# A fused attention, mixture and channel-mix kernel: the order of issue from a table in the source in place of the framework's scheduler

## The chip, the cores and the metric

The kernel runs on one core of a Trainium2 chip. The metric is the device time of one execution in microseconds (us), the median of several runs. Less is better.

## The reference

Three layers follow each other, with 4 batches, 544 rows per batch (32 "global" and 512 "local") and a model width of 512.

1. Attention with 8 heads of width 64. The 32 global queries see all 544 keys. A local query sees the 32 global keys and the local keys at most 32 places away.
2. A mixture of 4 experts, each a causal attention with its own `wq`, `wk`, `wv` of width 64 and an output weight `wo`. A gate picks the best two of four experts for each row and weighs them.
3. A channel mix: with `xk` and `xr` as blends of each row and the row before it, the result is `sigmoid(xr @ w_r) * (relu(xk @ w_k)**2 @ w_v)`, with a hidden width of 1024.

```
s = where(abs(i - j) <= 32, q_l @ k_l.T / 8, -1e9);  out_l = softmax([q_l @ k_g.T / 8, s]) @ [v_g, v_l]
x = concat([out_g, out_l]).transpose(0, 2, 1, 3).reshape(B, S, H * D)
ye = softmax(causal(scale * (x @ wq[e]) @ (x @ wk[e]).T)) @ (x @ wv[e]) @ wo[e]      # e = 0..3
x = sum over the two chosen experts of weight * ye
out = sigmoid(xr @ w_r) * (maximum(xk @ w_k, 0) ** 2 @ w_v)
```

All inputs and the output are float32.

## The kernel before, in words

The transposed activations `xT` of all four batches stay in SBUF. Precise products are made of three matmuls on a high and a low part (`mm3`, lines 112 to 114), plain float32 matmuls appear in the trace as two instructions each.

**Stage A** (lines 220 to 376) is the first attention. It goes over 32 half units `n`, a pair of heads and half of its queries each. `a_qk` makes scores S in eight matmuls on half of the array's rows each: head `h` = 0 uses rows 0 to 63, head 1 rows 64 to 127, and the program lists them in turns. VectorE (DVE) takes them out with a mask and a row minimum, ScalarE (ACT) makes the exponential, GpSimd (POOL) normalizes (`a_norm`), TensorE (PE) transposes (`a_tp`) and multiplies by the values (`a_pv`). For every fourth `n`, `g_qk` makes the scores of the global queries: for each pair and head a matmul of 512 columns into `Sga` and one of 32 columns into `Sgb`.

**Stage B/C** (from line 878, with `c_step`) is the mixture. `b_split` splits half a batch of `xT` into high and low parts in the one buffer `x`; `b_qk` and `b_v` make q, k and v of it. Then for each of 8 units per batch `c_qk` makes causal scores C of 128 to 512 columns (again in turns between the two row halves), DVE takes them out, ACT makes the exponential, POOL scales, PE transposes into `cT`, ACT and DVE copy that to `cpt`, and `c_pv` multiplies by the values into `y`. `e_wo` applies `wo` (tile `po`). Between these steps the 20 weight splits of the third layer (`load_wd`, `split_wd`) are placed, each with work on ACT, POOL and DVE.

**Stage D** is the channel mix over five blocks of tokens: `d_mix` makes blends on ACT, DVE and POOL; `d_k`, `d_v` and `d_r` are long runs of 128x512 matmuls; `d_out` multiplies and stores.

In the kernel before, the code only traces the operations. The framework's scheduler, with a model of time inside, then sets the order in which each engine issues them, and the allocator gives buffers in that order. At some places `tc.issue_after` ties an operation behind another one on its engine (`with after(last_act):` and the like). An engine issues its own instructions in order: one that waits for a semaphore holds up all behind it on that engine. The scores' and transposes' PSUM tiles share six buffers, `x` has one, most others two to four.

Of the kernel before, what the change touches and what calls it, by code (L numbers as in the profile page):

```python
# [23 lines left out]
W = 160  # L24
# [21 lines left out]
def v32(ap):  # L46
    return ap.bitcast(F32)


@with_exitstack  # L50
def chain_kernel(ctx: ExitStack, tc: tile.TileContext, kq, vw, vgd, wqkv, pack, wo, w_k, w_v, w_r, c_causal, out):
    nc = tc.nc

    const = ctx.enter_context(tc.tile_pool(name="const", bufs=1))
    sb = ctx.enter_context(tc.tile_pool(name="sb", bufs=1))
    xpool = ctx.enter_context(tc.tile_pool(name="xpool", bufs=1))
    tiny = ctx.enter_context(tc.tile_pool(name="tiny", bufs=1))
    ps = ctx.enter_context(tc.tile_pool(name="ps", bufs=1, space=PSUM))
    dr = ctx.enter_context(tc.tile_pool(name="dr", bufs=1, space=bass.MemoryType.DRAM))


# [93 lines left out]
    def split_wd(name, raw, c, k):  # L155
        lo, hi, hf = raw[:, :, 0], raw[:, :, 1], v32(raw)[:, :, 1]
        y = T("wy", [512], f"wy{name}{c}{k}", U32)
        g = T("wg", [512], f"wg{name}{c}{k}", U32)


        with after(last_act):
            nc.scalar.activation(v32(g), hf, AF.Sign, bias=tcol)
            nc.scalar.activation(v32(y), hf, AF.Abs)
        with after(last_pool):
            nc.gpsimd.tensor_scalar(v32(y), v32(y), TINY, None, op0=ALU.max)
        with after(last_dve):
            nc.vector.tensor_scalar(y, y, 3, 0x7fffffff, op0=ALU.logical_shift_left, op1=ALU.bitwise_and)
        nc.vector.scalar_tensor_tensor(g, lo, 29, g, op0=ALU.logical_shift_right, op1=ALU.bitwise_or)
        nc.vector.scalar_tensor_tensor(y, y, 0x7f800000, g, op0=ALU.bitwise_xor, op1=ALU.bitwise_xor)
        if name == "k":  # L170
            if (name, k) not in wd:
                for s in "HL":
                    place_wd(name, k, s)
            H_, L_ = [t[c % 4] for t in wd[name, k]]
        else:
            H_, L_ = g.bitcast(F32R), y.bitcast(F32R)
        nc.scalar.copy(H_, v32(y))
        nc.gpsimd.tensor_sub(L_, v32(y), v32(H_))
        if name != "k":
            for s, t in zip("HL", (H_, L_)):  # L180
                nc.sync.dma_start(wdr[name, k, s][:, c % 4], v32(t))
# [14 lines left out]
    def split_wb(step, c):  # L196
        kind = "qkv"[step]
        r = wraw[kind][:, c]
        H_, L_ = [t[:, c] for t in wqk[kind]]
        with after(last_act):  # L200
            nc.scalar.copy(H_, r)
        return lambda: nc.gpsimd.tensor_sub(L_, r, v32(H_))


# [27 lines left out]
        vws[P] = t  # L232

    def a_qk(n):
        nonlocal last_act, last_dve
# [12 lines left out]
        su = T("su", [4], f"su{n}", F32, 4)  # L248
        for i in range(2):
            k = 2 * j + i  # L250
            m = 0 if k == 0 else (2 if k == NB - 1 else 1)
            for h in range(2):
                c = 2 * h + i
                last_dve = nc.vector.tensor_tensor_reduce(out=ts[:, h, i], in0=st[h][:, i * W:(i + 1) * W],  # L254
                                                          in1=band[:, m], op0=ALU.add, op1=ALU.min, scale=-SCALE,
                                                          scalar=BIG, accum_out=mn[:, c:c + 1])
                last_act = nc.scalar.activation(ts[:, h, i], ts[:, h, i], AF.Exp, bias=mn[:, c:c + 1], scale=-1.0,  # L257
                                                accum_out=su[:, c:c + 1])
        sm[n] = ts
        rs[n] = su  # L260

    def a_norm(n):
        nonlocal last_pool
# [13 lines left out]
        g = glob[u][:, 2 * j:2 * j + 2, 2 * pp:2 * pp + 2, :].rearrange("p i h c -> p h i c")  # L277
        rb = rc.rearrange("p (h i) -> p h i", h=2)[:, :, :, None].to_broadcast([128, 2, 2, SG])
        last_pool = nc.gpsimd.tensor_tensor(g, t[:, :, 64:96].rearrange("p (h i) c -> p h i c", h=2), rb, op=ALU.mult)
        pn[n] = o  # L280

    def a_tp(n):
# [99 lines left out]
        return lambda: split_wo(raw)  # L382

    def split_wo(raw):
        with after(last_act):
            nc.scalar.copy(woS[0], raw)
        with after(last_pool):
            nc.gpsimd.tensor_sub(woS[1], raw, v32(woS[0]))
# [113 lines left out]
    csm, crs, cpt, ptl = {}, {}, {}, {}  # L502

    def c_qk(b, ep, i):
        nonlocal last_act
        w = 128 * (i + 1)
        q = qk[b, ep]
        rc = slice(i * 128, (i + 1) * 128)
# [16 lines left out]

    def c_norm(b, ep, i):
        w = 128 * (i + 1)
        nonlocal last_dve, last_pool
# [4 lines left out]
        last_dve = nc.vector.tensor_mul(rc, rc, gate[b][:, i, 2 * ep:2 * ep + 2])  # L533
        for e in range(2):
            t = csm[b, ep, i][e]
            last_pool = nc.gpsimd.tensor_tensor(t[:, :w], t[:, :w], rc[:, e:e + 1].to_broadcast([128, w]),  # L536
                                                op=ALU.mult)

    def c_tp(b, ep, i):
        nonlocal last_act, last_dve  # L540
        ts = csm.pop((b, ep, i))
        pt = T("cpt", [2, NB, 160], f"cpt{b}{ep}{i}")
        for e in range(2):
# [236 lines left out]
    def c_step(m):  # L780
# [27 lines left out]
        if m == MIX:  # L808
            d_begin()
        if MIX <= m < MIX + NC:  # L810
            with after(last_act), after(last_dve), after(last_pool):
                d_mix(0, 0, [m - MIX])
        if m >= K0 and m < K0 + FIRST:
            d_k(0, m - K0)
        if jobs and m >= J0 and (m - J0) % 4 < 3:
# [20 lines left out]
    for n in range(NU + 6):  # L836
        if n == 5:
            nc.sync.dma_start(small, pack)
        if n == 14:
            ql = T("ql", [2, 2, 128], "ql", F32R)  # L840
            qld = [[ql[:, p, s] for s in range(2)] for p in range(2)]
            with after(last_pool):
                nc.gpsimd.memset(v32(ql), 0.0)
            with after(last_dve):
                nc.vector.tensor_scalar(omu, mu, -1.0, 1.0, op0=ALU.mult, op1=ALU.add)
        u, r = divmod(n, 4)
        with after(last_pool):
            for g in low:
                g()
        low = []  # L850
        if n < NU:
            a_qk(n)
# [49 lines left out]
    for n, (g0, w) in enumerate(tokens):  # L902
# [24 lines left out]
        else:  # L927
# [78 lines left out]
```

## Time and profile before

| | |
|---|---|
| median of 3 runs | 560.54 us (559.16 to 562.76) |
| the profiled execution's own time | 559.32 us |
| its span, first to last instruction | 557.5 us |
| busy PE | 536.3 us (96%), 4286 matmuls |
| busy DVE | 323.1 us (58%) |
| busy ACT | 318.8 us (57%) |
| busy POOL | 299.6 us (54%) |
| moved by DMA | 50.98 MB, 91 GB/s |

The span is what lies between the first and the last instruction of the profiled execution; its own time has some 1.8 us more around it. A busy PE is one with a matmul in it, not one at its peak: matmuls overlap, and their ends are modelled. Stage A fills the first 140 us or so with work of stage B from about 60 us on, stage B/C runs from there to about 325 us, and stage D from there to the end.

### The profile page before, as it was taken

The numbers are of one execution on the slowest core, as the hardware profiler recorded it, in microseconds if no ns is written. First come the engines' busy times: TensorE is split into PE (matmuls) and PEld (weight loads), VectorE is DVE, ScalarE is ACT, GpSimd is POOL, SyncE is SP. The second block draws the span as 40 slices with busy tenths as digits, with TensorE's granted clock in tenths as the row PEclk, the third lists the DMA queues.
The fourth block names the chain that finished last, engine by engine and source line by source line (L and its number), as shares of the span: only waits on it lengthen the run. The fifth ranks groups of instructions, "written<-read, shape, count | busy, mean of one in ns | idle before, by whom it ended". The sixth has DMA issues, their size and how long they took to land.

```text
span 557.5 us, 11727 instructions
## 1 busy us (share of the span) xinstructions
PE 536.3 (96%) x4286; PEld 435.4 (78%) x4286; DVE 323.1 (58%) x1065; ACT 318.8 (57%) x891; POOL 299.6 (54%) x361
## 2 busy tenths in 40 slices
PE   6899999999898999899999999999999999999997
PEld 4577777889786888788776688888888888888885
DVE  3577865664799689979999751346134714431001
ACT  5789765764678586778679562265235734332211
POOL 5578844544468788868886841434244725312210
PEclk9799999999988999999999999999999999999999
DMA  8867543020134354333531220002000100110002
GB/s 349 315 238 250 167 141 127 3 79 19 39 116 150 114 192 150 114 115 114 178 132 69 76 76 2 0 1 76 1 0 17 59 2 0 39 38 20 0 1 75
DMA packets 16024, 50.98 MB, mean 91 GB/s; under 512 B 1760, under 2 KB 2400, under 8 KB 15328
## 3 DMA queue, kind: packets, MB, share of 16 engines
q1 hardware_dynamic: 15680, 49.98, 25.7%
q8 instruction: 34, 0.56, 0.4%
q10 hardware_dynamic: 288, 0.26, 0.1%
q14 instruction: 22, 0.18, 0.1%
HBM read 39.49 MB, written 10.75 MB: 90 GB/s over the span
## 4 chain that ended last, share of the span: by engine, by line
PE 77%; DVE 13%; ACT 4%; POOL 2%; issue 2%; DMA 2%; SPq 0%; DVEq 0%; POOLq 0%; ACTq 0%
PE k L113 6%; PE k L114 6%; PE k L112 6%; PE v L114 5%; PE v L112 5%; PE v L113 5%; PE S L244 5%; PE x L362 4%; PE pT L294 3%; PE r L114 3%; PE r L113 3%; PE r L112 3%; PE y L617 2%; DVE csm L518 2%; PE xg L368 2%
## 5 line engine op out<-in xcount | busy, mean ns | idle before, releaser
L718 POOL TENSOR_TENSOR kk<-k,kk 128x512 fp32r<-128x512 f32 x32 | 41.8, 1309 | 92.1 <-ACT kk L717 90.3
L709 DVE TENSOR_TENSOR k<-k 128x512 f32<-128x512 f32 x32 | 23.5, 738 | 98.2 <-ACT k L708 98.2
L693 DVE SCALAR_TENSOR_TENSOR mm<-xT,small,mt 128x32 f32<-128x32 f32 (+4 forms) x64 | 53.4, 880 | 30.7 <-POOL m1cpt L697 19.7
L257 ACT ACTIVATE sm<-sm,mn 128x160 f32<-128x160 f32 x128 | 53.4, 419 | 20.9 <-DVE mn L254 20.5
L536 POOL TENSOR_TENSOR csm<-csm,crc 128x128 f32<-128x128 f32 (+3 forms) x64 | 52.9, 847 | 19.1 <-DVE crc L533 14.2
L708 ACT ACTIVATE k<-k 128x512 f32<-128x512 f32 x32 | 18.9, 593 | 69.3 <-PE k L114 69.3
L275 POOL TENSOR_TENSOR pn<-sm,rc 128x256 f32<-128x256 f32 x64 | 38.0, 614 | 21.4 <-PE pT L294 15.2
L520 ACT ACTIVATE csm<-csm,cmn 128x128 f32<-128x128 f32 (+3 forms) x64 | 35.6, 559 | 9.2 <-DVE cmn L518 6.8
L244 PE MATMUL S<-kq 64*64 64x160 f32 x512 | 33.8, 335 | 5.7 <-DMA kq<-in_kq_dram 4.1
L692 ACT ACTIVATE mt<-xT,omu 128x32 f32<-128x32 f32 (+4 forms) x64 | 31.6, 518 | 13.0 <-DVE mm L693 12.9
L697 POOL TENSOR_TENSOR m1cpt<-mm,m1vC 128x512 fp32r<-128x512 f32 x16 | 20.6, 1300 | 33.4 <-ACT m1vC L696 33.4
L254 DVE CUSTOM_DVE_ANT_0 sm<-S,band 128x160 f32<-128x160 f32 x128 | 33.8, 315 | 5.7 <-PE S L244 5.5
L617 PE MATMUL y<-cpt,vC 128*64 128x128 f32 (+1 forms) x320 | 34.4, 301 | 2.1 <-ACT cpt L549 2.1
L697 POOL TENSOR_TENSOR m0L<-mm,m0H 128x512 fp32r<-128x512 f32 (+1 forms) x20 | 22.6, 1139 | 18.0 <-ACT m0H L696 17.9
L244 PEld LDWEIGHTS S<-kq 64*64 64x64 f32 x512 | 21.6, 147 | 13.2 <-DMA kq<-in_kq_dram 4.1
L717 ACT CAST kk<-k 128x512 fp32r<-128x512 f32 x32 | 19.9, 620 | 19.2 <-DVE k L709 19.2
L518 DVE CUSTOM_DVE_ANT_0 csm<-C,causal 128x128 f32<-128x128 f32 (+3 forms) x64 | 29.2, 483 | 2.2 <-PE C L120 1.9
L617 PEld LDWEIGHTS y<-cpt,vC 128*64 128x64 f32 x320 | 21.2, 138 | 11.9 <-issue 7.1
L546 PE MATMUL cT<-ident,csm 128*128 128x128 f32 x160 | 26.7, 282 | 3.3 <-POOL csm L536 1.5
L362 PE MATMUL x<-pt,vw 128*64 128x64 f32 x512 | 28.4, 233 | 0.0
L120 PE MATMUL C<-qk 64*128 64x128 f32 (+3 forms) x192 | 26.8, 354 | 1.0 <-DVE cmn L518 0.8
L362 PEld LDWEIGHTS x<-pt,vw 128*64 128x64 f32 x512 | 24.3, 138 | 4.2 <-issue 3.2
(403 smaller groups left out, 1735.0 us busy)
## 6 DMA issues: line engine op xcount, KB each, us to landing
kq<-in_kq_dram SPq DMA_DIRECT2D x15, 688.0 KB, 4.5
vw<-in_vw_dram SPq DMA_DIRECT2D x16, 512.0 KB, 5.7
out_dram<-rt SPq DMA_DIRECT2D x17, 256.0 KB, 2.0
wrawv<-in_moe_w_v_dram SPq DMA_DIRECT2D x8, 512.0 KB, 3.7
wrawk<-in_moe_w_k_dram SPq DMA_DIRECT2D x8, 512.0 KB, 3.6
wrawr<-in_moe_w_r_dram SPq DMA_DIRECT2D x4, 512.0 KB, 4.1
dv0H<-wgv SPq DMA_DIRECT2D x4, 256.0 KB, 2.4
dv0L<-wyv SPq DMA_DIRECT2D x4, 256.0 KB, 2.7
```

The lines of the kernel that those rows point to most:

```text
L112: nc.tensor.matmul(o, wH, xH, start=start, stop=False)
L113: nc.tensor.matmul(o, wH, xL, start=False, stop=False)
L114: nc.tensor.matmul(o, wL, xH, start=False, stop=stop)
L244: nc.tensor.matmul(st[h][64 * c:64 * c + 64, i * W:(i + 1) * W], t[rr, 64 * blk:64 * blk + 64], t[rr, KT0 + 96 * blk:KT0 + 96 * blk + W], ...
L257: last_act = nc.scalar.activation(ts[:, h, i], ts[:, h, i], AF.Exp, bias=mn[:, c:c + 1], scale=-1.0, accum_out=su[:, c:c + 1])
L362: nc.tensor.matmul(xs[pp][rr, 64 * blk:64 * blk + 64], w, pt[2 * pp + m // 2][:, 2 * h + m % 2, 64 * c:64 * c + 64], start=blk == 0, stop= ...
L518: nc.vector.tensor_tensor_reduce(out=t[:, :w], in0=st[e][:, :w], in1=causal[:, 512 - w:], op0=ALU.add, op1=ALU.min, scale=-SCALE, scalar=B ...
L536: last_pool = nc.gpsimd.tensor_tensor(t[:, :w], t[:, :w], rc[:, e:e + 1].to_broadcast([128, w]), op=ALU.mult)
L617: nc.tensor.matmul(yp[64 * e:64 * e + 64, o0:o0 + n], vC[b][:, j, hh * HD:(hh + 1) * HD], pt[:, e, j, 0:n], start=j == 0, stop=j == i and ...
L693: nc.vector.scalar_tensor_tensor(mm[:, cc], x, mu[:, kind, c:c + 1], mt[:, cc], op0=ALU.mult, op1=ALU.add)
L697: nc.gpsimd.tensor_sub(hl[1][c], mm[:, :w], v32(hl[0][c]))
L718: nc.gpsimd.tensor_sub(hl[1], k2, v32(hl[0]))
```

## The change

All operations are still written in the same order in the source, with the same shapes, engines, tiles and buffer counts. But `nc` is now a `Log` that only notes each call, 5354 in all, and tiles are made when an operation that uses them is issued (`Lazy`). All `issue_after` ties are gone. At the end the notes are issued to the framework one by one in the order of a table of numbers, inside `tc.manual_schedule()`, which keeps the order as given. The table is coded by differences: each word is a step from the number after the last one, with `xN` for N such steps.

```
+    def emit(self, order):
+        def now(x):
+            return x.get() if isinstance(x, Lazy) else x
+
+        for n in order:
+            engine, name, args, kwargs = self.ops[n]
+            getattr(getattr(self.nc, engine), name)(*[now(x) for x in args], **{k: now(x) for k, x in kwargs.items()})
...
 def chain_kernel(ctx: ExitStack, tc: tile.TileContext, kq, vw, vgd, wqkv, pack, wo, w_k, w_v, w_r, c_causal, out):
-    nc = tc.nc
-
-    const = ctx.enter_context(tc.tile_pool(name="const", bufs=1))
...
+    nc = Log(tc.nc)
+
+    const = LazyPool(ctx.enter_context(tc.tile_pool(name="const", bufs=1)))
...
-        with after(last_act):
-            nc.scalar.activation(v32(g), hf, AF.Sign, bias=tcol)
-            nc.scalar.activation(v32(y), hf, AF.Abs)
...
+        nc.scalar.activation(v32(g), hf, AF.Sign, bias=tcol)
+        nc.scalar.activation(v32(y), hf, AF.Abs)
...
+    with tc.manual_schedule():
+        nc.emit(sequence(ORDER))
+
+
+def sequence(text):
+    n = 0
+    for word in text.split():
+        step, _, count = word.partition("x")
+        n += int(step)
+        for _ in range(int(count or 1)):
+            yield n
+            n += 1
+
+
+ORDER = """
+0 17 1 584 -592 -13 16 -17 13 -2 -2 -4 8 -21 8 2 -3 10 -19 1x2 1 -2 190 -195 18x2 1 44 -50 49 -46x2 96 -97x4 -8 7x3 1
...
+22 -23x7 6 -7 6x2 -8 7 -8x2 12 -13 12 -8 7x2 -15 14
+"""
```

The table can be read without a chip: the calls are numbered as the source makes them. So the numbers 28 to 35 are the eight score matmuls of `n` = 0, in turns between the row halves, and 60 to 67 are `Sga`, `Sgb` of pair 0 head 0, then of pair 0 head 1, and so on. Engine by engine the table is not the order of the trace before. Counting calls on the same engine, 230 of 3357 keep their place on PE, 73 of 845 on DVE, 66 of 687 on ACT, 79 of 357 on POOL and 67 of 108 on SP's queue of DMAs; half of them move by at most 16 places on PE, 4 on DVE, 3 on ACT and 2 on POOL, the furthest by 135, 77, 164 and 56; on SP none moves by more than 9.

## Rows read from the trace of the kernel before

**Rows 1.** Busy PE, PEld, DVE, ACT, POOL by stretch; PE clock, DMA share, GB/s.
```profile
0.00:25.00 25.00, 17.86 (x175) 11.33 (x175) 11.14 (x80) 15.30 (x58) 12.07 (x32) 0.86 0.93 362
25.00:150.00 125.00, 124.89 (x1805) 98.95 (x1803) 81.68 (x431) 85.34 (x313) 71.89 (x120) 1.00 0.35 117
150.00:182.00 32.00, 28.50 (x214) 23.93 (x213) 30.27 (x104) 25.04 (x72) 25.69 (x28) 0.89 0.39 128
182.00:309.00 127.00, 120.39 (x970) 99.05 (x969) 110.28 (x330) 95.45 (x257) 101.03 (x109) 1.00 0.40 135
325.00:552.00 227.00, 227.00 (x1014) 188.32 (x1013) 76.04 (x104) 87.35 (x174) 78.09 (x65) 1.00 0.06 20
```

**Rows 2.** What idle PE waited for: us in total, times, longest.
```profile
PE S L244 <- DMA kq<-in_kq_dram: 4.1, 1, 4.1
PE pv L112 <- ACT x L399: 2.7, 2, 1.6
PE y L617 <- ACT cpt L549: 2.1, 2, 1.5
PE cT L546 <- POOL csm L536: 1.5, 1, 1.5
```

**Rows 3.** PE in order of time in stage A: start, duration, rows*columns of the array.
```profile
45.85 0.76 PE L244 MATMUL S<-kq 64*64 64x160 f32 x8
46.54 0.69 PE L362 MATMUL x<-pt,vw 128*64 128x64 f32 x16
47.15 0.76 PE L244 MATMUL S<-kq 64*64 64x160 f32 x8
47.84 1.08 PE L319 MATMUL Sga<-kq 64*32 64x512 f32 x8
48.73 0.26 PE L320 MATMUL Sgb<-kq 64*32 64x32 f32 x8
48.92 0.66 PE L294 MATMUL pT<-ident,pn 128*128 128x128 f32 x4
49.50 0.78 PE L244 MATMUL S<-kq 64*64 64x160 f32 x16
50.21 0.33 PE L294 MATMUL pT<-ident,pn 128*128 128x128 f32 x1
```

**Rows 4.** PE in order of time at a change of batch in stage C.
```profile
170.32 0.97 PE L120 MATMUL C<-qk 64*128 64x512 f32 x6
171.22 0.40 PE L112 MATMUL pb11k<-x,wk 128*128 128x288 f32 x1
...
172.92 0.60 PE L546 MATMUL cT<-ident,csm 128*128 128x128 f32 x4
173.45 0.44 PE L617 MATMUL y<-cpt,vC 128*64 128x128 f32 x4
...
175.96 0.39 PE L112 MATMUL pv<-wv,x 128*128 128x260 f32 x1 [1.58 <-ACT x L399]
```

**Rows 5.** ACT in order of time at the same place.
```profile
175.50 1.02 ACT L399 CAST x<-xT 128x256 fp32r<-128x256 f32 x3
```

**Rows 6.** The chain that ended last, in order of time: start, duration.
```profile
18.42 0.62 PE x L362 x8
...
492.94 0.87 PE kT L736 x8
```

**Rows 7.** PE in order of time at the end of stage C.
```profile
302.45 0.96 PE L120 MATMUL C<-qk 64*128 64x512 f32 x3
303.34 1.30 PE L617 MATMUL y<-cpt,vC 128*64 128x160 f32 x14
...
304.80 0.96 PE L120 MATMUL C<-qk 64*128 64x512 f32 x3
305.69 0.44 PE L617 MATMUL y<-cpt,vC 128*64 128x128 f32 x4
...
313.44 0.60 PE L546 MATMUL cT<-ident,csm 128*128 128x128 f32 x4
```

More of the change, by code (lines that the diff above doesn't have):

```diff
@@ L47, in v32, with __init__, get, shape @@
     return ap.bitcast(F32)
+class Lazy:
+    def __init__(self, make, view):
+        self.make, self.view, self.ap = make, view, None
+    def get(self):
+        if self.ap is None:
+            self.ap = self.make()
+        return self.ap
+    @property
+    def shape(self):
+        return self.view.shape
+    def __getitem__(self, key):
+        return Lazy(lambda: self.get()[key], None if self.view is None else self.view[key])
+    def rearrange(self, *args, **kwargs):
+        return Lazy(lambda: self.get().rearrange(*args, **kwargs), None)
+    def bitcast(self, dt):
+        return Lazy(lambda: self.get().bitcast(dt), self.view)
+    def to_broadcast(self, shape):
+        return Lazy(lambda: self.get().to_broadcast(shape), None)
@@ new lines, with __init__, tile, __getattr__ @@
+class LazyPool:
+    def __init__(self, pool):
+        self.pool = pool
+    def tile(self, shape, dt, **kwargs):
+        return Lazy(lambda: self.pool.tile(shape, dt, **kwargs), np.broadcast_to(np.float32(0), shape))
+class Log:
+    def __init__(self, nc):
+        self.nc, self.ops = nc, []
+    def __getattr__(self, engine):
+        return LogEngine(self, engine)
+    def emit(self, order):
[4 more added lines that the diff above has]
+            getattr(getattr(self.nc, engine), name)(*[now(x) for x in args], **{k: now(x) for k, x in kwargs.items()})
@@ L50, in chain_kernel, with __init__, __getattr__ @@
+class LogEngine:
+    def __init__(self, log, engine):
+        self.log, self.engine = log, engine
+    def __getattr__(self, name):
+        return lambda *args, **kwargs: self.log.ops.append((self.engine, name, args, kwargs))
 @with_exitstack
 def chain_kernel(ctx: ExitStack, tc: tile.TileContext, kq, vw, vgd, wqkv, pack, wo, w_k, w_v, w_r, c_causal, out):
-    nc = tc.nc
-    const = ctx.enter_context(tc.tile_pool(name="const", bufs=1))
-    sb = ctx.enter_context(tc.tile_pool(name="sb", bufs=1))
@@ L56, in chain_kernel @@
-    xpool = ctx.enter_context(tc.tile_pool(name="xpool", bufs=1))
-    tiny = ctx.enter_context(tc.tile_pool(name="tiny", bufs=1))
-    ps = ctx.enter_context(tc.tile_pool(name="ps", bufs=1, space=PSUM))
+    nc = Log(tc.nc)
+    const = LazyPool(ctx.enter_context(tc.tile_pool(name="const", bufs=1)))
+    sb = LazyPool(ctx.enter_context(tc.tile_pool(name="sb", bufs=1)))
+    xpool = LazyPool(ctx.enter_context(tc.tile_pool(name="xpool", bufs=1)))
+    tiny = LazyPool(ctx.enter_context(tc.tile_pool(name="tiny", bufs=1)))
@@ L59, in chain_kernel @@
+    ps = LazyPool(ctx.enter_context(tc.tile_pool(name="ps", bufs=1, space=PSUM)))
     dr = ctx.enter_context(tc.tile_pool(name="dr", bufs=1, space=bass.MemoryType.DRAM))
@@ L158, in split_wd @@
         g = T("wg", [512], f"wg{name}{c}{k}", U32)
-        with after(last_act):
-            nc.scalar.activation(v32(g), hf, AF.Sign, bias=tcol)
-            nc.scalar.activation(v32(y), hf, AF.Abs)
[L164 to L167, printed above, removed]
+        nc.scalar.activation(v32(g), hf, AF.Sign, bias=tcol)
+        nc.scalar.activation(v32(y), hf, AF.Abs)
+        nc.gpsimd.tensor_scalar(v32(y), v32(y), TINY, None, op0=ALU.max)
+        nc.vector.tensor_scalar(y, y, 3, 0x7fffffff, op0=ALU.logical_shift_left, op1=ALU.bitwise_and)
         nc.vector.scalar_tensor_tensor(g, lo, 29, g, op0=ALU.logical_shift_right, op1=ALU.bitwise_or)
@@ L199, in split_wb @@
         H_, L_ = [t[:, c] for t in wqk[kind]]
-        with after(last_act):
-            nc.scalar.copy(H_, r)
+        nc.scalar.copy(H_, r)
         return lambda: nc.gpsimd.tensor_sub(L_, r, v32(H_))
@@ L262, in a_norm @@
     def a_norm(n):
-        nonlocal last_pool
         u, r = divmod(n, 4)
@@ L384, in split_wo @@
     def split_wo(raw):
[L385 to L388, printed above, removed]
+        nc.scalar.copy(woS[0], raw)
+        nc.gpsimd.tensor_sub(woS[1], raw, v32(woS[0]))
     xHL, qk, vC, gate, lg = {}, {}, {}, {}, {}
@@ L504, in c_qk @@
     def c_qk(b, ep, i):
-        nonlocal last_act
         w = 128 * (i + 1)
@@ L810, in c_step @@
         if MIX <= m < MIX + NC:
-            with after(last_act), after(last_dve), after(last_pool):
-                d_mix(0, 0, [m - MIX])
+            d_mix(0, 0, [m - MIX])
         if m >= K0 and m < K0 + FIRST:
@@ L841, in chain_kernel @@
             qld = [[ql[:, p, s] for s in range(2)] for p in range(2)]
[L842 to L845, printed above, removed]
+            nc.gpsimd.memset(v32(ql), 0.0)
+            nc.vector.tensor_scalar(omu, mu, -1.0, 1.0, op0=ALU.mult, op1=ALU.add)
         u, r = divmod(n, 4)
-        with after(last_pool):
-            for g in low:
-                g()
+        for g in low:
+            g()
         low = []
@@ new lines @@
+126 -127x3 71 -72x3 -78 77x4 -25 -55 78 -79 78x3 -28 27 112 -113x2 -84 83 96x7 15 -16 -104 -90 89x7 54 -55 95 -96x2
+101 -102x8 44 -45 85 -86x3 41 -42 -80 79x2 41 -42 92 -90 75 -41 -10 49 -49 -33 37 14x2 -24 23x2 110 -111x2 109 -136
+25x3 107 -107 -18x2 -46 64 -20x2 67 -67 75 -60 59x2 -65 64 -125 43 -44 44 -45x2 108 -109 55 64 -121 109 -110x2 48
+-49x3 47 -48 23x2 54 -80 24x2 117 -77 12 -99 85 -43 37 4x2 85x2 -87 86x3 -96 -66 160x5 -22 21x3 -93 92 -89 88x3 -99
+98x9 -79x3 -31 30 -25x2 23 -24x4 57 -58x2 37x2 -37 36x2 -35 50 -17x2 -40 39x2 -45 9 229x2 -238 2 234x3 -194 193x3 -192
@@ new lines @@
+-8 -49 202x3 -162 161 -116x2 -42 41 -48 47 -107 106x5 -51 50x6 -96 -7 101x7 -66 65x2 -129 128 36 -37 -57x2 -17 16x2 58
+-2 1 29 -30 -61 146 -87 30 55 -87x4 85 -86x2 22 -23x2 131x2 -133x2 131 -113 112 -152 151 -152x2 131 -3 -114x2 109 4
+-115x4 111 -112x2 -24 25 20 -18 6x2 -12 -4 14x2 60 -74 73 31 -32 -63 52 9x2 -75 74x2 -15 14 -61 79 -20x3 -87 86 27x2
+-12 11x2 -242x2 125 -126 239 -240x3 205 -206 359 -360 225 -19 -208 204 20 -226 206 -207 356 -156 -202 358 -231x2
+-130x2 128 71 22 -95 4 28x4 -37 16x2 438 -439x2 438 -439 439 -440 -18 17x2 2 119x2 -118 117x2 -123 122x2 -111 110x2
```

136 lines of the change are left out of this document (122 added, 14 removed).

## The prediction

> **What bounds the kernel now.** I read the busy time by stretch first, then the waits of PE, then PE's order of time at the places where it waits, and last the order in the table, worked out by numbering the calls of the source and counting through the table's steps. The stretches [rows 1] show four regimes. From 0 to 25 us no engine is full: PE is busy for 17.9 us, at a mean granted clock of 0.86, and the DMA engines are at 0.93. From 25 to 150 PE is full (124.9 of 125) while DVE is at 65%: here PE's own work sets the time, and an order helps only if it makes that work shorter. From 150 to 309 PE stands idle for 10.1 us and DVE is busy for 140.6 of 159 us, 95% in 150 to 182: PE and DVE share the bound. From 325 to 552 PE is full with 128x512 matmuls (227.0 of 227): an order can't gain there, only lose. The waits of PE that have a name [rows 2] are few: the first load, the buffer `x` (2.7 us), `cpt` (2.1), `csm` (1.5).
>
> The profile's execution took 559.3 us, 0.2% under the median of 560.5; the sum is made against 559.3.
>
> **The change, part by part.** The same 5354 calls are issued; what moves is their order on five engines. I take the places where the two orders differ in a way that a row prices.
>
> *Row halves side by side, stage A.* Sixteen instructions of S that use both row halves in turns take 0.71 us (49.50 to 50.21), but a group of eight takes 0.69 (45.85 to 46.54, and again at 47.15) [rows 3]. So the eight have no partner: I read them as one head alone, then the other. The trace has twelve such groups, for six of the 32 units. In the table all 32 units stand whole and in turns. Each saves 2 x 0.69 - 0.71 = 0.67 us; five lie in 25 to 150, where PE is the bound: -3.4. The sixth lies before 25 us, where PE waits anyway: 0.
>
> *The same for C.* Six matmuls of 512 columns in turns take 0.90 us (170.32 to 171.22) [rows 4]; three alone take 0.89, twice (302.45 to 303.34 and 304.80 to 305.69) [rows 7]. Three units are cut so, one of them with 256 columns; in the table none is. That is 0.9 + 0.9 + 0.5 = 2.3 us of PE.
>
> *Sga and Sgb, against it.* Before, all `Sga` of a group stand together: eight instructions of 512 columns take 0.89 us, `Sgb` another 0.19 [rows 3], so two heads run side by side. In the table each `Sga` is followed by its own `Sgb` on the same row half, then comes the other head. If a matmul waits at the head of PE's queue until its half is free, the other head can't pass it: four steps of 0.44 in place of two, 1.78 for 1.08, +0.7 us for each of 8 groups. No row shows this order, so the bounds are 0 (the other half runs past) and 8 x 0.7 = 5.6. In [rows 3] the eight take two full steps, so a third matmul does wait for its half: I take the upper end for the six groups past 25 us, +4.2.
>
> A sentence of the Trainium skill weighs here: its page "TensorEngine Tiling (Array Packing)", "Restrictions and Gotchas", says that row tiles can't use one PSUM bank at the same time. Both heads of `Sga` write the one bank `Sga`, and the measured 0.89 for 8 x 512 columns says that they do run together, so I go by the row; by the page nothing could be lost here and the sum below would be 4.2 us lower.
>
> *Changes of the array's shape.* A change between 128*128, 128*64, 64*64 and so on costs time: four transposes before a `y` take 0.53 us (172.92 to 173.45) [rows 4], four of the run of eight `kT`, without change, 4 x 0.87 / 8 = 0.435 [rows 6], so about 0.09 us for a change. Counted over neighbours in PE's order there are 278 changes before and 194 in the table: 117 and 81 in what lies in 25 to 150, 148 and 100 after it. Ten and six of these belong to the halves above. That leaves 26 x 0.09 = -2.3 us in the first stretch and 42 x 0.09 = 3.8 us of PE in the second.
>
> So 25 to 150 changes by -3.4 - 2.3 + 4.2 = -1.5 us. In 150 to 325 PE's work shrinks by 2.3 + 3.8 = 6.1, but DVE is at 88%, and where DVE sets the pace a shorter PE only waits longer: I take half, -3.0 (bounds 0 and -6.1).
>
> *The hand-over of `x`.* The next half batch can be split into `x` only when the last q/k matmul has read it. At 175.96 PE waited 1.58 us for this, with the copies on ACT starting at 175.50 [rows 4, 5]. PE's work between the last reader and the first user of the new half, summed by each shape's own spacing, is 1.4 to 2.3 us at the six hand-overs after the first one before, and 2.9 to 5.0 in the table; on ACT the copies also stand two exponentials earlier at this batch. I take the 2.7 us [rows 2] as gone: -2.7. Late next is DVE.
>
> *The end of stage C and `cpt`.* Between the scores C and the transposes of the same unit PE has 3.5 to 6.1 us of other work in the last three units before; in the table `d_k` of five slices (13.6 us of 512-column matmuls) is pulled in between, and it is 8.8 to 17.2. The wait for `csm` goes, and one of the two for `cpt` (the place at 151.65, where cover grows from 0.6 to 1.6 us): -1.5 - 1.1. A wait for `cpt` comes back at three others, where the table has 0 to 0.4 us between the last transpose and `y`: priced by the 2.1 us for two [rows 2], 0.8 each, +2.4; behind it stands all of PE.
>
> *Clock and weight splits.* In 150 to 182 the clock was 0.89, after idle time [rows 1]. The table puts 4.7 us of DVE work (the first weight splits) ahead of the 512-column C of batch 0, into a stretch with DVE at 65%. 30.3 of 32 us of DVE become about 26, so PE should run on with less idle time; of the 28.5 x 0.11 = 3.1 us I take half, -1.5.
>
> *Costed at nothing.* DMAs: 108 issues, none moved by over 9 places. `vw0` goes behind `vw4` and five others; 4.8 MB at 362 GB/s [rows 1] are in by about 13 us, and PE first multiplies by it at 18.42 [rows 6]. Without that cover it would be one load, 1.4 us. Start: 0, between -4 (half of the idle 7.1) and +3 (`Sga` at a low clock). Stage D: the table issues up to eight slices of `d_k` before their `d_v`, and the work between a `d_k` and its `d_v` is never below 5.4 us, as before, or 2.7 in the short block, where only two copies lie between; 0, upper bound some 4.
>
> Sum: -1.5 - 3.0 - 2.7 - 2.6 + 2.4 - 1.5 = -8.9 in what is sized so far. 559.3 - 8.9 = 550.4, and I say **550.4 us**.
>
> **The rivals.**
>
> *More is gained* (539 us). If DVE's idle 18.4 us in 150 to 309 halve (-9), the start gives 4 and PE's 6.1 counts in full, the sum is near -20. For it: DVE has the work moved ahead, and C's cover grows from 10.5 to 12.2 us in the mean. Against it: the work of DVE up to each later batch stays within 3.4 us of before.
>
> *Waits only move* (559). DVE, ACT and POOL have the same instructions. If DVE sets the end of stage C, PE's shorter work there and the waits that go are worth nothing, and what is left is -1.5 and about +1.
>
> *Slower* (570). PE waits for the softmax in the middle of stage C. The chain from C to its transposes took 8.6 us at the end (304.80 to 313.44) [rows 7]. In the table nine units have less work between, 5.9 to 8.1 us, together 11.7 us short of that; before it was twelve units, but mostly at the end. If those nine come due in full, no other wait shrinks and the upper end of `Sga` counts: 559.3 - 5.7 + 5.6 + 2.4 + 11.7 - 3.0 = 570.3. It decides once the chain takes more than about 7 us with DVE loaded. For it: DVE at 95%. Against it: the first unit of batch 3 before had 5.4 us of cover and waited little.
>
> That the table repeats the old order is excluded by the counts: over 90% of PE's calls stand elsewhere.
>
> **How the numbers follow.** Forecast 0.44, more gained 0.17, waits only move 0.21, slower 0.18. The forecast's own bounds are 559.3 - 15 and 559.3 - 4, so nearly all of it is over 1% (about what a measurement here can tell from no change); with 0.02 of it within: faster 0.60, same 0.22, slower 0.18. For 8 in 10 the range reaches from 537, inside the more-gained case, to 569, just short of the slow one.
>
> **What would show it.** Right: S of all 32 units at 0.7 us in one piece; fewer breaks between shapes; `Sga` with `Sgb` at 1.8 us a group; no wait for `x` over 1 us; a full PE from 300 us on; DVE under 90% in the 32 us past the first 512-column C. Wrong: `Sga` at 1.1 us; PE idle between C and `cT` in the middle batches; any gap in stage D; a start in which PE is idle for longer than 7 us.

## The result, and the profile after

The changed kernel takes 554.55 us (median of 4 runs, 553.01 to 555.63) against 561.35 us for the kernel before in the same session: a ratio of 0.988, with a 95% interval of 0.9835 to 0.9926. That is 1.2% faster; the forecast was 550.4 against 559.3 (a ratio of 0.984), its range 537 to 569. The profiled execution took 553.6 us, its span is 551.8, 5.7 us shorter than before.

In the changed kernel one line (L100) issues everything, so its trace is read by tiles. The busy time by stretch of the kernel after, with the columns of [rows 1]:

```profile
25.00:150.00 125.00, 120.62 (x1751) 95.50 (x1748) 84.48 (x417) 88.48 (x313) 77.08 (x123) 1.00 0.41 133
150.00:182.00 32.00, 30.28 (x263) 25.20 (x262) 28.74 (x115) 23.34 (x70) 23.28 (x31) 1.00 0.24 76
182.00:309.00 127.00, 118.06 (x957) 101.08 (x956) 109.07 (x325) 96.66 (x258) 102.20 (x105) 0.95 0.39 134
```

Against [rows 1], PE is no longer full from 25 to 150 us (120.62 for 124.89), the clock of 150 to 182 is whole (1.00 for 0.89) and that of 182 to 309 is not (0.95 for 1.00). But equal times hold different work in the two kernels. So I cut both traces where PE has done the same amount of work, and split PE's time in three: work (from each matmul's start to the next one's, without idle time), the part of it that a low clock cost (half of the time spent at 1.2 GHz in place of 2.4), and idle time. Their bounds are about 30, 146 and 340 us before, and 29, 149 and 333 us after; each cell gives before to after.

| us | work | cost of the low clock | idle |
|---|---|---|---|
| start, behind the first load | 19.8 to 20.9 | 3.5 to 0 | 3.1 to 2.8 |
| rest of stage A | 115.9 to 115.9 | 0 to 0 | 0.1 to 4.4 |
| stage B/C | 180.1 to 167.7 | 3.4 to 6.3 | 10.1 to 10.8 |
| stage D | 213.7 to 213.9 | 0 to 0 | 0 to 0 |

The start gives 2.7 us (and the first load takes 0.8 of it back), the rest of stage A loses 4.3, stage B/C gives 8.8, stage D stands still.

What idle PE waited for, in the kernel after (us in total, times, longest), answers to [rows 2]:

```profile
PE pT L100 <- POOL pn L100: 2.4, 2, 1.5
PE cT L100 <- POOL csm L100: 2.0, 4, 0.8
PE C L100 <- ACT cpt L100: 1.9, 1, 1.9
PE C L100 <- DVE qk L100: 1.4, 1, 1.4
PE cT L100 <- DVE cpt L100: 1.2, 2, 0.8
PE y L100 <- DVE cpt L100: 1.0, 2, 0.6
PE y L100 <- ACT cpt L100: 0.7, 1, 0.7
PE y L100 <- POOL cpt L100: 0.4, 1, 0.4
```

The wait for `x` (2.7 us) has left the list and those of `y` for `cpt` are 2.1 us in total as before (1.0, 0.7 and 0.4), but the first five of these lines are new or longer.

PE in order of time in stage A of the kernel after answers to [rows 3]: a group whose two pairs stand apart, and one (from 44.11, its first lines) whose eight calls stand together.

```profile
29.66 1.05 PE L100 MATMUL Sga<-kq 64*32 64x512 f32 x4
30.55 0.23 PE L100 MATMUL Sgb<-kq 64*32 64x32 f32 x4
30.71 1.32 PE L100 MATMUL S<-kq 64*64 64x160 f32 x32
...
33.50 1.05 PE L100 MATMUL Sga<-kq 64*32 64x512 f32 x4
34.38 0.23 PE L100 MATMUL Sgb<-kq 64*32 64x32 f32 x4
...
44.11 1.04 PE L100 MATMUL Sga<-kq 64*32 64x512 f32 x2
45.04 0.19 PE L100 MATMUL Sgb<-kq 64*32 64x32 f32 x1
```

Four `Sga` instructions of one pair take 0.89 us (29.66 to 30.55), as long as the eight of both pairs in [rows 3]. So the pairs, which use different columns of the array, ran four abreast before, and only two abreast now: 2.1 us a group for 1.08. The two units of S at 30.71 show the other side: 1.32 us for 32 instructions, side by side throughout.

In stage C the same holds for `y`, which uses 64 columns for each of two experts. The unit with four key blocks, before (first three lines) and after:

```profile
187.43 0.49 PE L617 MATMUL y<-cpt,vC 128*64 128x160 f32 x2
189.45 0.76 PE L617 MATMUL y<-cpt,vC 128*64 128x160 f32 x6
191.99 0.76 PE L617 MATMUL y<-cpt,vC 128*64 128x160 f32 x8
```

```profile
301.63 1.31 PE L100 MATMUL y<-cpt,vC 128*64 128x160 f32 x16 [0.73 <-ACT cpt L100]
302.87 0.30 PE L100 MATMUL y<-ptl,vl 32*64 32x32 f32 x4
```

Before, the unit is cut 2 + 6 + 8 and takes 0.41 + 0.69 + 0.69 = 1.79 us to the next matmul in each place; the 2 and the 6 each hold a call without its partner. After, it is one run of 1.24 us. The trace before has 30 such runs of 2, 6, 10 or 18 instructions among 51 runs of `y`; after, all 28 runs are multiples of four.

Last, the clock. Busy time, with the granted clock third from the right, around the waits before (first four lines) and after:

```profile
150.00:153.00 3.00, 1.08 (x13) 0.73 (x11) 2.92 (x13) 3.00 (x10) 2.59 (x4) 1.00 0.34 132
153.00:157.00 4.00, 4.00 (x22) 4.00 (x22) 3.85 (x11) 1.77 (x6) 3.50 (x4) 0.57 0.44 131
174.00:177.00 3.00, 1.42 (x14) 1.14 (x13) 3.00 (x12) 2.98 (x11) 3.00 (x5) 1.00 0.65 214
177.00:181.00 4.00, 4.00 (x25) 3.11 (x24) 3.82 (x10) 3.99 (x13) 4.00 (x6) 0.57 0.44 131
```

```profile
218.00:221.00 3.00, 1.62 (x16) 1.25 (x16) 2.56 (x9) 1.40 (x5) 3.00 (x3) 1.00 0.44 146
221.00:228.00 7.00, 6.57 (x40) 4.43 (x41) 6.05 (x22) 4.79 (x16) 5.53 (x9) 0.51 0.20 76
268.00:272.00 4.00, 2.10 (x18) 1.74 (x17) 3.75 (x16) 3.66 (x10) 2.24 (x2) 1.00 0.86 315
272.00:279.00 7.00, 6.17 (x41) 4.66 (x40) 5.30 (x19) 4.17 (x14) 4.12 (x6) 0.52 0.69 274
```

In each of the four places PE stands idle for 1.4 to 1.9 us within 3 or 4 us, and then the clock is at its lower level, 1.2 GHz, for 3.4 us (before) or 6.8 us (after), which lies within the stretches of 4 and 7 us shown. The table removed both places of before and made two new ones, with longer falls behind them.

### The profile page after: what moved, and what is told of

Its sections match the earlier page's. It is cut to its first block, busy times and chain, and to the rows that moved or that the text cites. A ratio compares the mean times of both kernels' runs of the same rounds, so it can differ in the third digit from the quotient of the medians.

```text
span 551.8 us, 11621 instructions
## 1 busy us (share of the span) xinstructions
PE 524.6 (95%) x4286; PEld 429.8 (78%) x4286; DVE 319.5 (58%) x1065; ACT 318.6 (58%) x891; POOL 303.7 (55%) x361
## 4 chain that ended last, share of the span: by engine, by line
PE 78%; DVE 9%; ACT 7%; POOL 3%; issue 1%; DMA 1%; ACTq 0%; DVEq 0%; POOLq 0%
PE v L100 17%; PE k L100 16%; PE r L100 8%; PE x L100 4%; PE S L100 4%; PE po L100 3%; PE pv L100 3%; PE y L100 3%; PE cT L100 3%; PE Sga L100 3%; PE C L100 3%; PE pT L100 2%; POOL csm L100 2%; ACT csm L100 2%; PE xg L100 1%; ACT sm L100 1%
## 5 line engine op out<-in xcount | busy, mean ns | idle before, releaser
L100 POOL TENSOR_TENSOR kk<-k,kk 128x512 fp32r<-128x512 f32 x32 | 41.7, 1311 | 92.9 <-ACT kk L100 92.8
L100 DVE TENSOR_TENSOR k<-k 128x512 f32<-128x512 f32 x34 | 29.3, 864 | 85.1 <-ACT k L100 84.6
L100 ACT ACTIVATE sm<-sm,mn 128x160 f32<-128x160 f32 x128 | 53.5, 420 | 24.4 <-DVE mn L100 21.0
L100 DVE SCALAR_TENSOR_TENSOR mm<-xT,small,mt 128x32 f32<-128x32 f32 (+7 forms) x64 | 48.5, 798 | 24.1 <-POOL m1cpt L100 12.5
L100 POOL TENSOR_TENSOR csm<-csm,crc 128x256 f32<-128x256 f32 (+3 forms) x64 | 51.9, 828 | 17.5 <-DVE crc L100 11.6
L100 POOL TENSOR_TENSOR pn<-sm,rc 128x256 f32<-128x256 f32 x64 | 38.6, 617 | 16.3 <-PE pT L100 6.5
L100 ACT ACTIVATE k<-k 128x512 f32<-128x512 f32 x34 | 20.3, 596 | 44.1 <-PE k L100 37.5
L100 DVE CUSTOM_DVE_ANT_0 sm<-S,band 128x160 f32<-128x160 f32 x128 | 35.2, 318 | 18.1 <-PE S L100 17.7
L100 PE MATMUL v<-wv1H,kk 128*128 128x512 f32 x136 | 43.6, 389 | 0.0
L100 PE MATMUL v<-wv0H,kk 128*128 128x512 f32 x136 | 43.5, 389 | 0.0
L100 ACT ACTIVATE csm<-csm,cmn 128x128 f32<-128x128 f32 (+3 forms) x64 | 35.8, 564 | 13.3 <-DVE cmn L100 12.9
L100 ACT ACTIVATE mt<-xT,omu 128x32 f32<-128x32 f32 (+7 forms) x64 | 31.6, 519 | 14.6 <-DVE mm L100 14.4
L100 POOL TENSOR_TENSOR m1cpt<-mm,m1vC 128x512 fp32r<-128x512 f32 x16 | 21.7, 1374 | 30.9 <-ACT m1vC L100 23.1
L100 DVE CUSTOM_DVE_ANT_0 csm<-C,causal 128x128 f32<-128x128 f32 (+3 forms) x64 | 29.9, 483 | 8.8 <-PE cT L100 4.8
L100 ACT CAST kk<-k 128x512 fp32r<-128x512 f32 x32 | 19.4, 620 | 24.2 <-PE v L100 13.6
L100 PE MATMUL S<-kq 64*64 64x160 f32 x512 | 27.1, 317 | 6.4 <-DMA kq<-in_kq_dram 4.9
L100 POOL TENSOR_TENSOR m0L<-mm,m0H 128x512 fp32r<-128x512 f32 (+1 forms) x20 | 25.2, 1271 | 14.2 <-ACT m0H L100 14.1
L100 DVE TENSOR_TENSOR rt<-v,rt 128x512 f32<-128x512 f32 x17 | 11.6, 686 | 36.0 <-PE v L100 26.3
L100 PE MATMUL y<-cpt,vC 128*64 128x128 f32 (+1 forms) x320 | 30.0, 313 | 2.2 <-DVE cpt L100 1.0
L100 PE MATMUL cT<-ident,csm 128*128 128x128 f32 x160 | 27.4, 288 | 4.2 <-POOL csm L100 2.0
L100 POOL TENSOR_TENSOR glob<-sm,rc 128x128 f32<-128x128 f32 x32 | 12.8, 403 | 33.9 <-DVE rc L100 23.1
L100 PEld LDWEIGHTS v<-wv0H,kk 128*128 128x128 f32 x136 | 25.5, 188 | 5.3
```

What stands on the lines that cost most here:

```text
L100: getattr(getattr(self.nc, engine), name)(*[now(x) for x in args], **{k: now(x) for k, x in kwargs.items()})
```

## The experiments

The theory after the comparison: (1) PE's own work sets the time, and it grows wherever halves of the array stand empty, by rows or by columns; (2) the table wins at S, C and `y` by keeping partners together and loses at `Sga`, where it takes them apart; (3) the waits of stage C only move. The rivals: the reading in the prediction that turns of `Sga` and `Sgb` do the harm; that DVE paces stage C; that the issue from a table is worth something by itself.

Runs e1 to e4 shared one chip, e5 to e8 another, e9 and e10 a third. So ratios to the kernel before compare across chips, medians only within one. The parts of PE's time, worked out as above:

| run | median us | ratio (95%) | stage A work, idle | B/C work, low clock, idle |
|---|---|---|---|---|
| before | 561.35 | 1 | 115.9, 0.1 | 180.1, 3.4, 10.1 |
| after | 554.55 | 0.988 (0.9835 to 0.9926) | 115.9, 4.4 | 167.7, 6.3, 10.8 |
| e1 | 543.55 | 0.9685 (0.9658 to 0.9712) | 110.0, 2.1 | 168.0, 4.8, 11.5 |
| e2 | 543.21 | 0.9684 (0.9656 to 0.9712) | 108.9, 1.8 | 167.6, 6.4, 10.8 |
| e3 | 559.74 | 0.9977 (0.9958 to 0.9997) | 115.9, 8.3 | 168.0, 4.8, 10.6 |
| e4 | 563.06 | 1.0022 (1.0 to 1.0044) | 115.8, 1.6 | 179.6, 6.8, 10.1 |
| e5 | 539.72 | 0.9601 (0.9563 to 0.9639) | 108.9, 1.9 | 167.6, 3.4, 10.8 |
| e6 | 547.13 | 0.9729 (0.9694 to 0.9764) | 108.9, 2.1 | 175.2, 4.8, 9.4 |
| e7 | 543.79 | 0.9666 (0.9632 to 0.9701) | 108.8, 1.9 | 168.6, 3.3, 12.0 |
| e8 | 552.58 | 0.982 (0.9775 to 0.9866) | 114.6, 2.3 | 168.0, 6.1, 11.5 |
| e9 | 541.97 | 0.9642 (0.9606 to 0.9678) | 108.9, 1.9 | 167.4, 6.3, 10.8 |
| e10 | 551.87 | 0.9814 (0.9776 to 0.9852) | 114.8, 1.1 | 167.9, 6.2, 11.1 |

**e1 and e2: the pairs of Sga together.**

```
-        nc.emit(sequence(ORDER))
+        nc.emit(joined(sequence(ORDER), range(8)))                      # e1
+        nc.emit(joined(sequence(ORDER), (0, 2, 4, 6, 1, 3, 5, 7)))      # e2
+GLOBAL = (60, 177, 378, 579, 781, 1023, 1257, 1497)
+def joined(order, calls):
+    order = list(order)
+    for g in GLOBAL:
+        i = max(order.index(g), order.index(g + 4))
+        group = [g + c for c in calls]
+        order = [n for n in order[:i] if n not in group] + group + [n for n in order[i:] if n not in group]
+    return order
```

> The table of the changed kernel, but the eight calls of a group of Sga and Sgb stand together, at the place of the later pair and in the source's order, Sga and Sgb in turns; in six of the eight groups the table has the two pairs apart. Theory (pairs): what lengthened Sga from 10.4 to 17.7 us of PE is that its two pairs, which use different columns of the array, no longer run side by side; together they cost about 1.1 to 1.3 us a group again in place of 1.9, so 4 to 6 us of PE go and the time is 548 to 551 against 554.5. Rival (turns, the reading of the prediction): each Sgb holds up the other head; the turns are still there, so a group stays at 1.8 and the time at 554 to 555. Rival (chain): stage A is paced by the softmax chain, PE only waits longer, 554 to 555 with Sga short.

> As the run before, but in each group the four Sga stand ahead of the four Sgb. Theory (pairs): only a group in which Sgb itself waits for its buffer can gain by it, such as group 3, which stood together and still took 2.0 us; 0 to 1.5 us less than the run before, 547 to 550. Rival (turns): all of the gain comes here and none before, 549 to 550 against 554 to 555.

Measured: 543.55 and 543.21, 2% below the changed kernel by their ratios. The forecast of 548 to 551 was too high, but the theory of the pairs holds and that of the turns falls: with turns and without, the time is the same. The turns are not even new. The order that e4 issues is the one of the kernel before, and in it the calls 378 to 385 stand as in the source, each `Sgb` right behind its `Sga`. In the trace before, the eight `Sga` of this group start together all the same:

```profile
34.59 1.08 PE L319 MATMUL Sga<-kq 64*32 64x512 f32 x8
```

The groups of tiles from 25 to 150 us, of the kernel before, the kernel after and e1 (busy us, mean ns):

```profile
L244 PE MATMUL S<-kq 64*64 64x160 f32 x400 | 24.1, 309 | 0.1
L319 PE MATMUL Sga<-kq 64*32 64x512 f32 x48 | 6.5, 601 | 0.0
```

```profile
L100 PE MATMUL S<-kq 64*64 64x160 f32 x384 | 19.8, 307 | 1.2 <-DVE mn L100 0.9 <-ACT ptlg L100 0.2
L100 PE MATMUL Sga<-kq 64*32 64x512 f32 x48 | 12.4, 601 | 0.0
```

```profile
L100 PE MATMUL S<-kq 64*64 64x160 f32 x384 | 18.3, 306 | 0.0
L100 PE MATMUL Sga<-kq 64*32 64x512 f32 x48 | 7.7, 601 | 0.0
```

The mean of one `Sga` is 601 ns in all three; only how many run at once differs. Between the profiled executions (553.6 and 543.55) 7.4 us are PE work, 6.0 of it in the rest of stage A; 1.5 are the clock and 1.2 waits. That S and the waits of stage A fell too was not expected. Most of it is one place of the kernel after, two units of S from 67.52 that take 2.40 us of PE, with a wait of 0.89 us between them and one of 0.87 behind. The second unit:

```profile
69.60 1.28 PE L100 MATMUL S<-kq 64*64 64x160 f32 x16 [0.89 <-DVE mn L100]
```

In e1 the two stand from 62.37, take 1.32 us, and one wait of 0.36 is left behind them. Which of the moved calls did that was not taken apart.

**e3 and e10: the old order of stage A, the table behind it.**

```
+        nc.emit(hybrid(list(sequence(BEFORE)), list(sequence(ORDER)), 1900))      # e10: 1700
+def hybrid(before, after, count):
+    return sorted(after[:count], key=before.index) + after[count:]
+BEFORE = """
...
```

> The first 1900 of the 5354 calls of the table (those up to about 142 us) are put into the order that the kernel before had, all later calls stand as in the table. Theory: the table loses in stage A (PE reaches the same amount of work 2.4 to 3.9 us later by 127 us) and gains some 8.6 us behind it, independently; so 550.5 to 552.5. Rival: the gain behind is only what stage A had put off; then the two cancel and it is 554 to 556, or more.

> The run with the first 1900 calls in the old order had a wait of 8.2 us at the seam. Here the cut is at 1700 calls (about 126 us), where the two orders have done the same calls but for six. Theory (the gain behind stage A does not depend on stage A's order; the table's stage A loses 2 to 4 us): 550 to 553 against 554.5. Rival (PE's work in stage A is 115.9 us in both orders, and the two lose alike): 554 to 556. Rival (the calls behind the seam wait for what the old order has late): 557 or more.

Measured: 559.74 for e3, the number of its rival, but not for the rival's reason. PE's work in stage B/C is 168.0, as in the table, so the gain there is not something that stage A had put off. What cost is the cut: one wait of 8.2 us at the seam, in PE's waits of e3, behind which the clock fell as well.

```profile
PE pvl L100 <- DVE xlH L100: 8.2, 1, 8.2
```

With the cut at a place where both orders have done nearly the same calls, e10 takes 551.87, as the theory has it: the old stage A has nearly the same PE work (114.8 for 115.9) but fewer waits (1.1 us for 4.4). More than half of that gain is lost again at the start, where the profiled execution of e10 has a fall of the clock (15.4 to 25.6 us) that the kernel after does not have. Its interval overlaps the changed kernel's, so the gain over the table rests on the trace more than on the times.

**e4: the old order from a table.** The edit replaces the table by one of the order of the kernel before.

> The mechanism of the change without its order: the calls are issued from a table, but in the order of the kernel before on every engine (four ACT copies at the end of stage C may stand in another order among themselves). Theory: only the order counts, 559.5 to 562.5 as before. Rival: that the ties between instructions and the scheduler's own placing are gone is worth something by itself, 555 to 558.

Measured: 563.06, a ratio of 1.0022 (1.0 to 1.0044). The issue from a table, with the ties gone, is worth nothing, or costs 0.2%; the gain comes from the order.

**e5 and e9: waits taken out by hand**, on top of e2. A call in brackets is put right behind the call after it (e5); e9 moves 13 more calls ahead.

```
+MOVES = (([3504], 3503), ([3429, 3479], 3504), ([3474], ...), ([2879], 2878), ([2775], 2879))
+# e9, ahead of: 55 of 104, 111 and 112 of 68, 92, 93, 113 and 114 of 94, 2885 of 2751,
+#     3449 of 3504, 3450 and 3474 of 3355, 3467 of 3479, 3468 of 3419
```

> The table with the groups of Sga and Sgb joined (four Sga first; 543.2 us), and three copies moved ahead on their engine: the ACT copy of cT2120 ahead of an exponential and a weight step, the DVE copy of cT2111 by three calls, the DVE subtraction that ends qk21 ahead of one gate step. PE waited for these 1.91, 0.78 and 1.38 us, and 2 to 3 us after the first and the last of these waits its granted clock was at 0.5 for some 7 us each. Theory (wait and clock): without the waits the low clock goes too, so 4 us of waits and up to 7 us of clock: 532 to 537. Rival (wait alone): 539 to 540. Rival (the next late producer takes over, since ACT and DVE do the same work): 542 to 543.5.

> The table of the run with three waits mended (539.7 us there), and the calls moved ahead on their engine for which PE waited next: 55 on ACT, 111 and 112 on DVE, 92, 93, 113 and 114 on POOL (PE's two waits for pn at the start, 0.86 and 1.54 us); 2885 on DVE (1.68); 3449 and 3467 on ACT, 3450, 3474 and 3468 on DVE (0.69 and 2.34). Theory (the low clock follows PE's idle time; waits can be taken out one by one): up to 7 us of waits, and 3.4 us for the low clock that is left: 531 to 536. Rival (the sum of waits stays near 11 us in stage C whatever is moved, as it did in all runs so far, and only the clock moves): 537 to 540.

Measured: 539.72 for e5, 4.1 us below e7 (the same time as e2) on the same chip, and the number of the rival "wait alone". But the trace says something else. In e2 these three waits are as in the kernel after: C for `cpt` 1.9 us, C for `qk` 1.4, `cT` for `cpt` 1.2. PE's longest waits of stage B/C in e5 (first two lines) and e9:

```profile
PE cT L100 <- DVE cpt L100: 2.8, 3, 1.7
PE C L100 <- DVE qk L100: 2.3, 1, 2.3
```

```profile
PE y L100 <- ACT cpt L100: 2.2, 2, 1.5
PE C L100 <- ACT cpt L100: 2.1, 1, 2.1
```

The waits that go are replaced by others of about the same size near the same places, for the next copy that is late: idle time in stage B/C is 10.8 us in e2, e5 and e9. What e5 has won is clock: the falls behind the two places are shorter, in e2 (first two lines) and e5.

```profile
210.00:217.00 7.00, 6.59 (x41) 4.42 (x40) 6.06 (x22) 4.79 (x16) 5.51 (x9) 0.51 0.20 76
261.00:269.00 8.00, 7.18 (x49) 5.66 (x50) 5.74 (x20) 4.82 (x16) 4.70 (x6) 0.57 0.59 230
```

```profile
211.00:215.00 4.00, 4.00 (x34) 3.12 (x32) 3.22 (x18) 3.80 (x14) 3.91 (x8) 0.57 0.31 114
262.00:266.00 4.00, 4.00 (x31) 3.42 (x30) 2.78 (x11) 2.27 (x10) 2.39 (x4) 0.57 0.64 259
```

The clock of all executions says the same. The mean granted clock of the six of e5 is 0.990 to 0.994, 0.9928 on average, of the six of e7 0.984 to 0.987, 0.9855 on average; 0.0073 of 540 us is 3.9 us (an estimate), nearly all of the 4.1. In e7's profiled execution the fall that e5 lacks lies at the start (13.4 to 20.3 us); its stage B/C has 3.3 us of low clock, as e5 has 3.4.

In e9 the longer falls are back, with the same idle time, and so is about half of the time (541.97; by the ratios e5 and e9 can't be told apart). So e5 is the fastest version here, 4% below the kernel before, but its last step over e2 is clock and not fewer waits. Why its falls are shorter is not shown.

**e6: partners of y apart**, on top of e2: in 15 units the calls of the second expert go behind the next run.

```
+MOVES = (([2009], 2026), ([2299], 2305), ([2554], 2538),
...
+         ([3691, 3692], 3747), ([3853, 3854], 3880))
+def moved(order, moves):
+    for calls, behind in moves:
+        order = [n for n in order if n not in calls]
+        i = order.index(behind) + 1
+        order[i:i] = calls
+    return order
```

> The joined table (543.2 us), but in 15 of the 32 units of stage C (eight of one key block, seven of two) the y matmuls of the second expert of a pair stand behind the next run of PE work, so the two experts, which use different columns of the array, are apart. A run of two calls takes 0.37 us and one of four 0.59 in the trace of the changed kernel, and a single call took 0.37 before: apart each unit costs its 0.37 or 0.59 once more, 8 x 0.37 + 7 x 0.59 = 7.1 us of PE. Theory (PE's own work counts in full in stage C): 549 to 552. Rival (DVE sets the pace there, half of it counts, the step of the prediction): 546 to 547.5. Rival (the column halves of calls that are apart run side by side all the same): 543 to 544.

Measured: 547.13, 3.3 us above e7 on the same chip, within the range of the rival that half of it counts. PE in order of time in e6, two units:

```profile
162.20 0.43 PE L100 MATMUL y<-cpt,vC 128*64 128x128 f32 x2
162.56 0.55 PE L100 MATMUL C<-qk 64*128 64x128 f32 x6
163.04 0.43 PE L100 MATMUL y<-cpt,vC 128*64 128x128 f32 x2
163.40 0.55 PE L100 MATMUL cT<-ident,csm 128*128 128x128 f32 x3
163.88 0.65 PE L100 MATMUL y<-cpt,vC 128*64 128x128 f32 x4
164.46 0.62 PE L100 MATMUL C<-qk 64*128 64x256 f32 x6
165.01 0.65 PE L100 MATMUL y<-cpt,vC 128*64 128x128 f32 x4
```

A run of two takes 0.36 us, twice, where the four together take 0.37 in the kernel after; a run of four 0.58, twice, where the eight together take 0.59. PE's work in stage B/C grows by 7.6 us, near the forecast (7.1). But idle time and low clock shrink by 1.4 and 1.6 us against e2 in this execution, and about half of it reaches the time. So in stage C PE's work does not count in full, and theory (1) holds there by half. That DVE's pace is the reason is not shown: part of what is given back is clock, and no run makes DVE's work shorter.

**e7 and e8: the heads of S in another order, and apart**, on top of e2.

```
+        nc.emit(by_head(joined(...)))       # e7: in each unit of S the calls 0, 2, 4, 6, then 1, 3, 5, 7
+MOVES = (([127, 129, 131, 133], 70), ([161, 163, 165, 167], 156),      # e8, 14 units: head 0 ahead of the run before
...
```

> The joined table (543.2 us), but in each of the 32 units of S the four matmuls of head 0 stand ahead of the four of head 1, in place of in turns; nothing comes between them. Theory (only what stands between counts; PE lets the other row half run): a unit stays near 0.7 us, 543 to 545. Rival (order in the queue counts: the second matmul of a head holds up the other head): up to 0.67 us for each of some 27 units in the full stretch, 556 to 562.

> The joined table (543.2 us), but in 14 of the 32 units of S the four matmuls of head 0 stand ahead of the PE run before, so that transposes or q/k matmuls come between the heads, as the kernel before had it for six units. Theory (the price of the prediction's first step): 14 x 0.67 = 9.4 us and up to 28 more changes of shape at about 0.09, 2.5: 552 to 555. Rival (PE has slack in stage A): 543 to 547.

Measured: 543.79 for e7, no change; 552.58 for e8, 8.8 us above e7 on the same chip, at the lower edge of the forecast. Some 2 of these are clock (0.982 on average for 0.9855, estimated as for e5). In the profiled executions S takes 7.4 us more of PE's work in e8, 0.53 us a unit where the forecast had 0.67. A unit of S in e7 (first line), one in e8 (the other two):

```profile
47.50 0.89 PE L100 MATMUL S<-kq 64*64 64x160 f32 x16
```

```profile
46.41 0.76 PE L100 MATMUL S<-kq 64*64 64x160 f32 x8
47.11 0.66 PE L100 MATMUL pTG<-ident,pg 128*128 128x128 f32 x4
47.70 0.76 PE L100 MATMUL S<-kq 64*64 64x160 f32 x8
```

By head but with nothing between, 0.82 us (47.50 to the next matmul at 48.32), and S as a whole takes 17.5 us in stage A past the start, as in e2 (17.4). With four transposes between the heads, 0.70 + 0.69.

## Why the prediction was right, and where it was not

The direction and the size were right (forecast -8.9, measured -5.7 in the profiled executions), the mechanism behind the first step was right, and three steps were wrong in part. That these made up for each other, and the number came out near, is in part luck.

- **S in one piece**: right. Forecast -3.4 past 25 us; past the start (30 us) S went from 21.3 to 18.8 us of PE work, -2.5, and to 17.2 in e1, where the place at 67.52 is mended. e8 puts the price back, 0.53 us a unit.
- **C in one piece**: right, and a little small: forecast 2.3, C went from 22.5 to 19.3.
- **Sga and Sgb**: right in sign, wrong in mechanism and too small. The prediction held that an `Sgb` at the head of the queue keeps the other head from passing. e1 and e7 refute that. And the turns are not new, as the line at 34.59 shows: the prediction took the order of the starts in the trace for the order of issue. The cost is that the table puts the two pairs of a group at two places, in six of eight groups: 5.9 us past the start in place of 4.2, and 2.1 more in the start. Its row was read wrongly: "the eight take two full steps" meant four abreast, by rows and by columns, and so the place of each pair in the table, which can be counted without a chip, was the thing to look at.
- **Changes of shape**: consistent, with no run of its own. `cT` went from 22.0 to 18.6, and the four `pTG` of e8 take 0.59 us between two S (47.11 to 47.70), near the 0.53 and 0.435 of [rows 4, 6].
- **A step that was missed**: partners of `y`, 32.4 to 27.1 us. The term for PE's work in 150 to 325 was 6.1, of which half was taken; it was 12.4. Of these, 8.8 us reached the time. e6 shows that `y` apart costs PE the work that the lengths of its runs say, and that about half of it reaches the time.
- **The hand-over of x, the end of stage C, cpt, the clock**: together forecast at -4.4 in 150 to 325. The wait for `x` went, as forecast. That of `cT` for `csm` went at the end of the stage and came back at four places (1.5 to 2.0 us), those of `y` for `cpt` stayed at 2.1, and new ones came. The sum of waits in stage B/C rose from 10.1 to 10.8 and the low clock's cost from 3.4 to 6.3. In this the rival "waits only move" was right, not in its time: the sum is 9.4 to 12.0 us in all twelve runs.
- Both errors together: 150 to 325 was forecast at about -7.4 with these terms and gave -8.8.
- **25 to 150**: forecast -1.5, measured +4.3 (cut at 30 and 146 us before). PE's work there did not change (-2.5 for S, +5.9 for `Sga` and `Sgb`, and -3.4 for all else, where the prediction had -2.3 for shapes), and 4.3 us of new waits were not foreseen: the prediction took a stretch with a full PE before for one with a full PE after.
- **Start**: forecast 0, measured -1.9, most of it a fall of the clock that this execution did not have. Such a fall is in all four profiled executions with the start of before (before, e3, e4, e10) and in two of eight with the table's (e2, e7), so the order may have a part in it; with one execution each that is not shown.
- **Stage D**: 0, and 0.2 measured, no gap.
- **The slower rival** did not come: the wait of `cT` for `csm` is 2.0 us in four places, not 11.7 in nine.

## What to carry to other kernels

Before an order is changed, list for every matmul that uses part of the array which other one shares the rest of it, by rows and by columns, and check that nothing stands between them: in this kernel one edit that joined six groups was worth some 10 us, 6 of them in the joined matmuls themselves, and the places can be counted in the source. Price such a step from the length of runs that hold a partner and runs that don't. In stage B/C of this kernel a wait that was moved came back as another one; of PE's work that was removed or added there, between 0.4 (e6) and 0.7 (the change) reached the time. In stage A, with PE full, it counted whole or nearly so (e1, e8).

## What the runs showed of the hardware

- Four matmuls on different parts of the array (two row halves, four column quarters) run at once into the one PSUM tile `Sga`: eight instructions of 512 columns take 0.89 us, four also 0.89, and the two of one call alone 0.93 (44.11 to 45.04).
- A matmul on another part of the array passes one that waits for its own part. In the table `Sgb` of head 0 stands ahead of `Sga` of head 1; in the trace all four `Sga` of the pair come first (29.66) and the `Sgb` 0.89 us later. In the group at 44.11, whose first `Sgb` also waits for its buffer, nothing passes until that `Sgb` starts at 45.04. So it holds for PE only in part that an engine issues its instructions in order, as is said ahead of the prediction. Whether a step of the build behind the table has a part in the new order was not separated. The page "TensorE: Matmul & The Clock Gate" of the Trainium skill, "Part 3: Packing small matmuls", says that matmuls are strictly first in, first out in their starts; this trace does not agree, and e7, which by that rule would have lost up to 0.67 us a unit, lost next to none (S 17.5 us in stage A past the start, for 17.4 in e2).
- At the four places shown the clock fell to 1.2 GHz 0.5 to 1.9 us after the end of a wait of 1.4 to 1.9 us, and stayed there for 3.4 or 6.8 us. One such fall costs half its length, as much as the wait before it or twice. Not every such wait has a fall behind it: before, the 1.55 us at 306 us have none, while the same wait in e4 (1.56 us at 309.6) has one of 3.4 us. What sets the length is not shown: the two long falls of the kernel after have 0.4 and 0.8 us of idle time inside, one of e4 (179.2 to 186.0 us) and one of e9 (211.9 to 218.7) have none.
